# Sketched attention and a squared-ReLU FFN on one core: query features turned in place instead of sent through DRAM

## The chip, the cores and the metric

The kernel runs on one core of a Trainium2 chip. The metric is the device time of one execution in microseconds (us), from several runs of the same kernel, of which the median counts. One further execution was taken by the hardware profiler. Engines: PE multiplies matrices, DVE and ACT are the two engines that can read PSUM and do elementwise work, POOL (GpSimd) works on SBUF alone, SP issues DMAs. DMAs are issued from the queues of SP, ACT and POOL.

## What is computed

There are 4 batch elements with 4 heads, 1088 tokens and a head dimension of 32. A row x has features phi(x): the outer product of S1 x (8 numbers) and S2 x (8 numbers), so 64 products. The attention is linear in these features, and its output goes through an FFN with a squared ReLU:

```python
def phi(x):
    a = np.einsum('rd,bhsd->bhsr', S1, x)
    b = np.einsum('rd,bhsd->bhsr', S2, x)
    return np.einsum('bhsi,bhsj->bhsij', a, b).reshape(*x.shape[:-1], r * r)
q_p, k_p = (phi(q), phi(k))
kv = np.einsum('bhsf,bhsd->bhfd', k_p, v)
z = np.sum(k_p, axis=2)
num = np.einsum('bhsf,bhfd->bhsd', q_p, kv)
den = np.einsum('bhsf,bhf->bhs', q_p, z)[..., None] + 1e-06
x = (num / den)            # heads side by side: (4352, 128)
h = x @ w_in               # 128 -> 2048
out = np.maximum(h, 0.0) ** 2 @ w_out
```

The attention part is in f32, the FFN in bf16.

## The kernel before, in words

The tokens are cut into nine chunks. Chunks 2b and 2b+1 are 512 tokens each of batch element b; chunk 0 is done in two halves, 0a and 0b; chunk 8 (the "rest") has the last 64 tokens of each element, 256 in all. Token j of a partition row is taken as 34 blocks of 32.

**Keys** (`k_stage`, L470; for element 0 the code at L385 to L424). DVE turns k in 32x32 blocks (L473), PE multiplies it by S1 and S2 (L479, L492), DVE turns the result back into token-major order (L484, L497) and makes the 64 products per token and head, kp (L504 in two instructions of 1024, L510 for the last 64 tokens). `z_stage` (L427) sums the factors for the denominators and gives Wc, a third projection whose product with the first one sums to the denominator. `kv_stage` (L449) multiplies kp by v (L456), copies the result (kvs), transposes it on PE (L466) and copies it to KV. For element 0 two of the products run on POOL.

**Queries, token-major** (`token_major`, L543; elements 0 and 1 and the rest). PE projects q to three sets (L555). ACT copies the first, qa. DVE multiplies it by the third (L563), sums it to the denominators (L566), takes the reciprocal (L567), scales qa by it (L569) and makes the products qo, two instructions of 512 for four groups of 128 tokens (L575). PE transposes qo in 128x128 pieces (L583), ACT copies the result to qp, PE multiplies qp by KV to x (`x_mm`, L535; the matmuls are L539), and ACT or DVE copies x to bf16, xT.

**Queries, compact** (`q_stage`, L622; elements 2 and 3). PE projects q feature-major (L633), the result is copied to qab, and `spread` (L608) stores it to DRAM (db on ACT's queue) and loads it back with every row repeated (QB, in two loads on SP's queue). The denominators come by a multiplication (L644), two PE steps (L650, L666) and a reciprocal (L658); the scaled factor, apr (L670), goes the same road through da to QA. DVE multiplies QA by QB to qp for each of two chunks (L679), and `x_mm` follows.

**FFN** (`f_stage`, L689). For each chunk, PE makes h from x and w_in (L707) into two PSUM buffers of two banks, ACT applies the ReLU to 1024 columns at a time (L710), DVE squares 2048 at a time (L714; in chunks 0a, 0b and 1 it may be ACT), and PE multiplies by w_out into one PSUM bank (L721, or L724 in token-major form for chunks 0a, 0b, 1 and 8). r and g have three buffers each. `store_turned` (L731) has DVE turn the output (L734) and SP store it in four DMAs; `store_rows` and `store_rest` copy it and store it.

**Order.** All of this is written as operations with an engine (or a choice of ACT and DVE), an estimated duration, what they read and write, and due times. `Plan.run` sets an order with these by list scheduling, and the instructions are issued in that order, so that each engine's queue is fixed. Three PSUM banks, t, are shared by all attention work, and early work may take the h banks as well (kind "r"). Ahead of the first FFN matmul, fillers (matmuls of zeros, L814) are put into gaps that the plan sees on PE. The first loads are on SP's queue; w_in, w_out and all later loads are on POOL's, behind the `gate` (L369), a small copy on POOL that waits for the first part of q.

Of the kernel before, what the change touches and what calls it, by code (L numbers as in the profile page):

```python
# [17 lines left out]
class Op:  # L18
    __slots__ = ("eng", "fn", "name", "preds", "succs", "dma", "base", "dl", "allocs", "frees", "n", "start", "end", "lead", "pri")
# [6 lines left out]
HOP, DELTA, FIX, TAIL, AHEAD = 0.08, 0.03, 1.4, 0.6, 9.9  # L26
FRAC = 0.94
RATE = 205.0


class Plan:
# [13 lines left out]
    def op(self, eng, dur, fn, reads=(), writes=(), name="", frees=(), dma=None, base=None, lead=0.0, pri=None):  # L45
# [3 lines left out]
        o.frees = list(frees)  # L49
# [40 lines left out]
    def run(self, slots, stretch=1.3, t0=0.7):  # L90
# [7 lines left out]

        left = {o: len(o.preds) for o in self.ops}
        ready = {o for o in self.ops if not o.preds}  # L100
        order = []
        while ready:
            best = {}
            for o in sorted(ready, key=lambda o: o.n):
                if any(not places(t) for t in o.allocs):
                    continue
                slot = max([min(places(t))[0] + HOP for t in o.allocs], default=0.0)
# [23 lines left out]
            if o.dma is not None:  # L131
                q_, x_ = ("SW", "HW") if e == "POOL" else ("HW", "SW")
                begin = max(dmat.get(q_, 0.0), o.end + FIX)
# [8 lines left out]
            for t in o.frees:  # L142
                pool[t.kind].append((s + d, (t.kind, t.i)))
# [19 lines left out]
def kernel(  # L163
# [64 lines left out]
    zs = ring("zs", 2, [128, H, r])  # L228
    KVs = [T(f"KV{b}", [128, 128]) for b in range(B)]
    x0 = T("x0", [128, 512], BF16)  # L230
# [4 lines left out]
    qp = ring("qp", 2, [128, 2, 512])  # L235
    den = ring("den", 2, [128, 32])
# [5 lines left out]
    QA = ring("QA", 2, [128, 2, 1024])  # L242
    QB = ring("QB", 2, [128, 2, 1024])
# [23 lines left out]
    def copy(name, eng, o, i, reads, writes, frees=(), lead=0.0):  # L267
# [4 lines left out]
        op(e, 0, lambda en: act.copy(o(), i()) if en == "ACT" else dve.tensor_copy(o(), i()),  # L272
           reads, writes, name, frees=frees, lead=lead)
# [66 lines left out]
    for i in range(2):  # L340
# [22 lines left out]
        in1=m4[:, None, :, None].to_broadcast([128, 2, H, r]), op=ALU.mult), [tp, "m4"], ["Wab"], "Wab", frees=[tp])  # L363
# [5 lines left out]
    op("POOL", 0.2, lambda e: pool.tensor_copy(gate, Q0[:1, 0, :8]), [f"{Q0k}.0"], ["gate"], "gate", pri=-190.0)  # L369
    load("POOL", "ld w_in", w_in, moe_w_in, 1049, ["w_in"], ["gate"], first=True)  # L370
    load("POOL", "ld w_out", w_out, moe_w_out.rearrange("(c ct) d -> c ct d", ct=CT), 1049, ["w_out"], ["gate"])
# [15 lines left out]
    def k1(m0, m1, Pn, key, nm):  # L387
# [3 lines left out]
        def mm(e):  # L391
            for m in range(n):
# [5 lines left out]
             lambda: pb(t)[:Pn, : 64 * n].rearrange("p (g a i) -> p g a i", a=2, i=r), [t], [f"kabz.{nm}"],  # L398
             frees=[t] if nm == "r" else [])
        for p0 in range(0, n, 2):  # L400
# [3 lines left out]
            def fn(e, p0=p0, p1=p1, w=w):  # L404
# [11 lines left out]
               [f"kabz.{nm}"] + ([] if onp else [t]), [f"{kp0k}.{m0 + p0}"], f"kp0.{m0 + p0}",  # L416
               frees=[t] if p0 == (0 if nm == "0" else 2) and not onp else [])
# [9 lines left out]
    def z_stage(b, keys, feat):  # L427
        t = tmp("r" if b == 0 else "t")

        def mm(e):  # L430
# [9 lines left out]
           [t, "mh"], [zk], f"zs{b}", frees=[t])  # L440
# [3 lines left out]
        copy(f"Wc{b}", "any", lambda: Wt[b][:, 2], lambda: pb(t2)[:, :32], [t2], [f"Wt{b}.c"], frees=[] if b in COMPACT else [t2])  # L444
        if b in COMPACT:
            W_, Wk = WQc(b)
            copy(f"WQc{b}", "any", lambda: W_, lambda: pb(t2)[:, :32].rearrange("p (x c i) -> p c i x", x=2, c=2), [t2], [Wk], frees=[t2])

    def kv_stage(b, parts):  # L449
# [12 lines left out]
        ks, ksk = kvs(b)  # L462
        copy(f"kvs{b}", "any", lambda: ks.rearrange("p (c f) -> p c f", c=2),
             lambda: pb(tv)[:, None, :64].to_broadcast([128, 2, 64]), [tv], [ksk], frees=[tv])
# [76 lines left out]
    ntok = [0]  # L541
# [308 lines left out]
```

## Time and profile before

| what | us |
|---|---|
| median of 3 runs | 125.84 (125.04 to 126.44) |
| the profiled execution, its own time | 124.5 |
| its span, first to last instruction | 122.4 |
| busy: PE, DVE, ACT, POOL | 109.1, 89.5, 84.8, 14.4 |
| first FFN matmul | 16.98 |
| relu, 68 of them (L710) | 66.5 |
| squares on DVE, 32 of them (L714) | 38.8 |
| end of the last FFN matmul | 117.4 |

The granted PE clock was 0.997 of full speed. The DMA queue of SP carried 8.10 MB. The span is the part that the profile's views divide up; 2.1 us of the execution's time lie around it. A group of instructions is named by line, engine, operation and what it writes and reads; the view of waits names the engine that waited, its line, and the engine and line that ended the wait, with the total, the count and the longest.

### The profile page before, as it was taken

The numbers are of one execution on the slowest core, as the hardware profiler recorded it, in microseconds if no ns is written. First come the engines' busy times: TensorE is split into PE (matmuls) and PEld (weight loads), VectorE is DVE, ScalarE is ACT, GpSimd is POOL, SyncE is SP. The second block draws the span as 40 slices with busy tenths as digits, with TensorE's granted clock in tenths as the row PEclk, the third lists the DMA queues.
The fourth block names the chain that finished last, engine by engine and source line by source line (L and its number), as shares of the span: only waits on it lengthen the run. The fifth ranks groups of instructions, "written<-read, shape, count | busy, mean of one in ns | idle before, by whom it ended". The sixth has DMA issues, their size and how long they took to land.

```text
span 122.4 us, 2878 instructions
## 1 busy us (share of the span) xinstructions
PE 109.1 (89%) x1170; PEld 67.7 (55%) x1170; DVE 89.5 (73%) x139; ACT 84.8 (69%) x116; POOL 14.4 (12%) x32
## 2 busy tenths in 40 slices
PE   6999998999998999999994599999979999999530
PEld 4688876947676369663452146455524355547420
DVE  4554797797998669999740999975869896774900
ACT  2431279999799638879779176779893989899510
POOL 3089413310002500000000000000000000000000
PEclk9999999999999999999999999999999999999998
DMA  2999999684013452444499145567950050230051
GB/s 75 270 202 185 247 408 257 137 260 181 12 48 86 124 197 65 110 110 102 105 229 191 45 110 131 111 121 161 200 76 0 0 86 0 35 56 0 16 92 24
DMA packets 19612, 14.88 MB, mean 122 GB/s; under 512 B 13968, under 2 KB 17552, under 8 KB 19088
## 3 DMA queue, kind: packets, MB, share of 16 engines
q1 hardware_dynamic: 17120, 8.10, 31.6%
q0 software_dynamic: 1728, 6.06, 18.0%
q10 hardware_dynamic: 752, 0.55, 1.5%
q8 instruction: 9, 0.15, 0.5%
q14 instruction: 3, 0.02, 0.1%
HBM read 13.00 MB, written 2.75 MB: 129 GB/s over the span
## 4 chain that ended last, share of the span: by engine, by line
PE 40%; DMA 17%; DVE 16%; ACT 13%; issue 10%; DVEq 0%; ACTq 0%
ACT r L710 11%; PE h L707 9%; DMA da<-apr 8%; DVE g L714 7%; PE o_ps L721 7%; PE o_ps L814 7%; DMA QA<-da 6%; PE t L539 3%; PE o_ps L724 3%; DMA out_dram<-osb 2%; DVE kp L504 2%; PE t L555 2%; PE h L456 1%; ACT qp L272 1%; PE t L633 1%
## 5 line engine op out<-in xcount | busy, mean ns | idle before, releaser
L710 ACT ACTIVATE r<-h 128x1024 bf16<-128x1024 f32 x68 | 66.5, 1027 | 11.4 <-PE h L707 11.1
L714 DVE TENSOR_TENSOR g<-r 128x2048 bf16<-128x2048 bf16 x32 | 38.8, 1214 | 7.7 <-ACT r L710 7.6
L707 PE MATMUL h<-xT,w_in 128*128 128x512 bf16 (+1 forms) x128 | 34.3, 371 | 0.5 <-ACT r L710 0.3
L707 PEld LDWEIGHTS <-w_in 128*128 128x128 bf16 x160 | 20.6, 149 | 10.8 <-issue 4.0
L721 PE MATMUL o_ps<-g,w_out 128*128 128x512 bf16 x96 | 24.7, 379 | 0.3 <-DVE g L714 0.2
L721 PEld LDWEIGHTS <-w_out 128*128 128x128 bf16 x96 | 9.0, 97 | 11.8 <-issue 3.2
L539 PE MATMUL t<-qp,KV 64*32 64x512 f32 (+2 forms) x96 | 8.7, 456 | 3.7 <-DVE qp L679 3.7
L724 PE MATMUL o_ps<-w_out,g 128*128 128x128 bf16 x160 | 10.6, 219 | 1.4 <-DVE osb L734 1.2
L724 PEld LDWEIGHTS <-g 128*128 128x128 bf16 x160 | 9.4, 98 | 3.0 <-DVE g L714 1.2
L814 PE MATMUL o_ps<-zero 128*128 128x256 bf16 x47 | 9.0, 335 | 1.2 <-DVE zero L338 1.2
L279 POOL DMA_DIRECT2D vin<-in_v_dram x12 | 6.7, 562 | 21.3 <-PE t L456 13.5
L679 DVE TENSOR_TENSOR qp<-QA,QB 128x1024 f32<-128x1024 f32 x4 | 4.9, 1220 | 5.9 <-DMA QA<-da 4.8
L504 DVE TENSOR_TENSOR kp<-kab 128x1024 f32<-128x1024 f32 x6 | 7.3, 1210 | 0.0
L814 PEld LDWEIGHTS <-zero 128*128 128x128 bf16 x47 | 5.2, 119 | 3.3 <-DVE zero L338 1.2
L575 DVE TENSOR_TENSOR qo<-qaq,t 128x512 f32<-128x512 f32 x9 | 6.0, 684 | 0.2
L734 DVE STREAM_TRANSPOSE osb<-o_ps 128x512 f32<-128x512 f32 x6 | 4.3, 710 | 1.8 <-PE o_ps L721 1.8
L539 PEld LDWEIGHTS t<-qp,KV 64*32 64x32 f32 x96 | 1.8, 105 | 6.9 <-issue 5.0
L583 PE MATMUL t<-ident,qo 128*128 128x128 f32 x32 | 4.8, 278 | 0.2
L707 PE MATMUL h<-x,w_in 128*128 128x256 bf16 x32 | 4.5, 272 | 0.2 <-ACT r L710 0.2
L272 ACT COPY qp<-t 128x512 f32<-128x512 f32 x8 | 4.5, 597 | 0.2 <-PE t L583 0.2
L456 PEld LDWEIGHTS t<-kp,vin 128*32 128x32 f32 (+1 forms) x216 | 3.3, 109 | 2.3 <-issue 2.3
L555 PE MATMUL t<-Wt,qT 128*128 128x96 f32 x32 | 4.5, 279 | 0.0
(107 smaller groups left out, 104.7 us busy)
## 6 DMA issues: line engine op xcount, KB each, us to landing
out_dram<-osb SPq DMA_DIRECT2D x32, 64.0 KB
QB<-db SPq DMA_DIRECT2D x4, 512.0 KB
QA<-da SPq DMA_DIRECT2D x2, 1024.0 KB
kin<-in_k_dram POOLq DMA_DIRECT2D x3, 544.0 KB, 8.3
qin<-in_q_dram POOLq DMA_DIRECT2D x3, 544.0 KB, 4.2
vin<-in_v_dram POOLq DMA_DIRECT2D x6, 144.0 KB, 7.1
vin<-in_v_dram POOLq DMA_DIRECT2D x6, 128.0 KB, 4.7
kin<-in_k_dram SPq DMA_DIRECT2D x2, 256.0 KB
```

The costliest lines, as they stand in the source:

```text
L272: op(e, 0, lambda en: act.copy(o(), i()) if en == "ACT" else dve.tensor_copy(o(), i()), reads, writes, name, frees=frees, lead=lead)
L279: op(eng, 0.5 if eng != "POOL" else 0.8, lambda e: qs[eng].dma_start(out=o, in_=i), reads, writes, name, dma=kb / RATE, pri=seq[0] - 200.0 ...
L504: dve.tensor_tensor(out=kp_[:, 4 * u : 4 * u + 4].rearrange("p m h i j -> p (m h) i j"), in0=x, in1=y, op=ALU.mult)
L539: pe.matmul(o[32 * h : 32 * h + 32, cs], kv_of(b, h), q_[64 * c : 64 * c + 64, x, cs], start=True, stop=True)
L555: pe.matmul(o[p0 : p0 + w, :, g], lhs, Wt[b], start=True, stop=True)
L575: dve.tensor_tensor(out=qo_[:, y : y + 2].rearrange("p g h i j -> p (g h) i j"), in0=x_, in1=y_, op=ALU.mult)
L707: pe.matmul(hv[:, x], w_inv[:, ct], X, start=True, stop=True)
L710: op("ACT", ACT(1024), lambda e, hv=hv, Rv=Rv, u=u: act.activation(Rv[:, KT * u : KT * u + KT], hv, ACTF.Relu), [f"h{hh}"], [f"{Rk}.{u}"], ...
L714: lambda e, R=R, G=G: dve.tensor_mul(G, R, R) if e == "DVE" else act.activation(G, R, ACTF.Square),
L721: pe.matmul(ob[:, :N], w_out[:, ct], Gv[:, y], start=(ct == 0), stop=(ct == CT - 1), skip_group_check=True)
L724: pe.matmul(ob[:, 128 * tt : 128 * tt + 128], Gv[:, y, tt * 128 : tt * 128 + 128], w_out[:, ct], start=(ct == 0 and tt == 0), stop=(ct == ...
L814: pe.matmul(ob[:, :256], zero[:, :128], zero[:, :256], start=True, stop=True)
```

## The change

Elements 1, 2 and 3 all take a new road, `turned_element`; `q_stage` is called no more, so db, da, QA and QB are gone.

- Features are made token-major as before, in two halves of four groups. Instead of PE's transposes and ACT's copies, DVE turns qo in 32x32 blocks into qd (`turned`), one instruction of 1024 for a half.
- x comes from `x_turned`: on 32x32 tiles of PE, four row groups (32 tokens each of a group of 128) by four column groups (heads), the 64 features in two parts that add up in PSUM. It works in two parts u, each with two row groups v, which write to two PSUM banks; each bank is copied to half of one chunk. This needs KV with its features repeated for the four row groups, KV4, made by two PE transposes. The tokens of an element's two chunks are thereby interleaved, and the stores are changed to match: eight DMAs of 32 KB a chunk instead of four of 64 KB.
- The rest takes this road too (REST4); it has a matmul for each group of 32 tokens. Element 0 gets KV4 beside KV.
- Key products of elements 1 to 3 (kp) all run on POOL: four instructions of 512 and one of 256 for the last tokens. kv is issued in four pieces instead of two.
- The first half of chunk 0 (`first_part`) makes its products without the denominators. These are computed beside it, spread by PE (R0.0), copied to Rs by ACT, and multiplied into x on the way out of PSUM, on DVE.
- The gate waits for the second part of k, and no longer for q.
- The plan: new constants and due times; a PSUM buffer is free when its last user has run, instead of at an operation that names it; fillers are put only into gaps of more than 0.07.

```diff
-HOP, DELTA, FIX, TAIL, AHEAD = 0.08, 0.03, 1.4, 0.6, 9.9
-FRAC = 0.94
-RATE = 205.0
+HOP, DELTA, FIX, TAIL, AHEAD = 0.08, 0.0, 1.4, 0.6, 10.0
+FRAC = 0.76
+RATE = 235.0
...
-STRETCH, BASE0, STEP = 1.28, 19.0, 10.36
+STRETCH, BASE0, STEP = 2.12, 16.9, 9.57
 TOK = ("0a", "0b", "1", "8")
 SQA = ("0a", "0b", "1")
-COMPACT = (2, 3)
-LEAD = [12.9, -0.6, -0.4, -0.9, 1.7, 4.2, 2.2, -3.0, 3.3]
+COMPACT = ()
+TURNED = (1, 2, 3)
+KPP = 5
+REST4 = True
+LATE = True
+LEAD = [10.9, -1.2, -0.8, 11.5, 3.0, 3.7, 3.5, -2.5, -15.0]
...
-    op("POOL", 0.2, lambda e: pool.tensor_copy(gate, Q0[:1, 0, :8]), [f"{Q0k}.0"], ["gate"], "gate", pri=-190.0)
+    op("POOL", 0.2, lambda e: pool.tensor_copy(gate, K0[:1, 4, :8]), [f"{K0k}.1"], ["gate"], "gate", pri=-190.0)
...
+        if blocks:
+            k4, k4k = kvs4(b)
+            copy(f"kvs4{b}", "any", lambda: k4,
+                 lambda: pb(tv)[:, :64].rearrange("p (y f) -> p y f", y=2)[:, :, None, :].to_broadcast([128, 2, 4, 32]),
+                 [tv], [k4k])
...
+        def turn4(e):
+            for y in range(2):
+                pe.transpose(pb(t4)[:, 128 * y : 128 * y + 128], k4[:, y].rearrange("p c f -> p (c f)"), ident)
...
-            op("DVE", DVE(1024), fn, [kbk], [f"{kpk}.{4 * u}"], f"kp{b}.{4 * u}")
+            op(*(("POOL", 1.12) if u < KPP else ("DVE", DVE(512))), fn, [kbk], [f"{kpk}.{2 * u}"], f"kp{b}.{2 * u}")
...
-        op("DVE", DVE(256), fnr, [krk], [f"{kpk}.8"], f"kp{b}.8")
+        op(*(("POOL", 0.64) if KPP > 4 else ("DVE", DVE(256))), fnr, [krk], [f"{kpk}.8"], f"kp{b}.8")
         z_stage(b, [kbk, krk], lambda m, a: (kr[:, a] if m == 8 else kb_[:, a, m]))
-        kv_stage(b, [([0, 1, 2, 3], f"{kpk}.0"), ([4, 5, 6, 7], f"{kpk}.4")])
+        kv_stage(b, [([m, m + 1], f"{kpk}.{m}") for m in range(0, 8, 2)])
...
+    def first_part(X, Xk):
...
+        op("DVE", DVE(512), fn, [qak, t], [f"{qok}.0", f"{qok}.2"], "qo0.0")
...
+        op("PE", 0.5, lambda e: x_mm(pb(tx), 0, q_, slice(0, 256)), [f"{qk}.0", "KV0"], [tx], "x0.0")
...
+        op("PE", 0.46, lambda e: [pe.matmul(pb(t3)[32 * h : 32 * h + 32, 128 * g : 128 * g + 128], dn[:, 4 * g + h : 4 * g + h + 1].to_broadcast([128, 32]), ident,
+                                            start=True, stop=True) for g in range(G) for h in range(H)], [dnk, "ident"], [t3], "R0.0")
+        copy("Rs0.0", "ACT", lambda: Rs, lambda: pb(t3)[:, :256], [t3], ["Rs"])
+        op("DVE", DVE(256), lambda e: dve.tensor_tensor(out=X, in0=pb(tx)[:, :256], in1=Rs, op=ALU.mult), [tx, "Rs"], [Xk], "xT0.0")
...
+    def turned(nm, qo_, keys, g0, G):
+        qd_, qdk = qd(0)
+        op("DVE", DVT(256 * G), lambda e: dve.transpose(
+            qd_[:, g0 : g0 + G].rearrange("p g f t -> p (g f t)"), qo_[:, :G].rearrange("p g h x y -> p (g h x y)")),
+           keys, [f"{qdk}.{g0}"], f"qd{nm}")
+        return f"{qdk}.{g0}"
+
+    def x_turned(nm, G, elem, qks, outs, lead):
+        qd_, _ = qd(0)
+        bs = sorted({elem(rg, g) for rg in range(4) for g in range(G)})
+        one = len(bs) == 1
+        n = 32 * G
+        for u in range(2):
+            banks = [tmp(), tmp()]
+
+            def part(e, u=u, banks=banks):
+                for g in range(1 if one else G):
+                    for y in range(2):
+                        for v in range(2):
+                            rg = 2 * u + v
+                            rows = slice(32 * rg, 32 * rg + 32)
+                            for h in range(H):
+                                o = pb(banks[v])[32 * h : 32 * h + 32, :n]
+                                pe.matmul(o if one else o[:, 32 * g : 32 * g + 32], KV4[elem(rg, g)][rows, y, 32 * h : 32 * h + 32],
+                                          qd_[rows, :G, 2 * h + y, :] if one else qd_[rows, g, 2 * h + y, :],
+                                          start=(y == 0), stop=(y == 1))
+
+            op("PE", (0.11 * G + 0.1) if one else 0.5, part, qks + [f"KV4{b}" for b in bs], banks, f"x{nm}.{u}")
+            for v in range(2):
+                X, Xk = outs[v]
+                copy(f"xT{nm}.{'AB'[v]}{u}", "any", lambda X=X, u=u: X[:, n * u : n * u + n], lambda v=v, banks=banks: pb(banks[v])[:, :n],
+                     [banks[v]], [f"{Xk}.{u}"], lead=lead)
+
+    def turned_element(b):
+        qt, qtk = qT(b)
+        keys = []
+        for u in range(2):
+            parts = [(g, 0, qt[:, 512 * u + 128 * g : 512 * u + 128 * g + 128], b) for g in range(4)]
+            qo_, ks_ = token_major(f"{b}.{u}", parts, 4, None, None, ([(b, None, None)], [(0, 0, f"{qtk}.{x}") for x in range(3)]), "turned")
+            keys.append(turned(f"{b}.{u}", qo_, ks_, 4 * u, 4))
+        x_turned(str(b), 8, lambda rg, g: b, keys, [xT(2 * b), xT(2 * b + 1)], LEAD[2 * b])
...
+                for x in range(4):
+                    for u in range(2):
+                        load("SP", f"st o{nm}.{x}{u}", o[:, u, :, 32 * x : 32 * x + 32], osv[32 * x : 32 * x + 32, u], 0.3 * N, [], [ok])
...
-                while t is not None and t < o.start < first + 0.01:
+                while t is not None and t + 0.07 < o.start < first + 0.01:
                     pe.matmul(ob[:, :256], zero[:, :128], zero[:, :256], start=True, stop=True)
-                    t += 0.22 if t < 4.5 else 0.11
+                    t += 0.215 if t < 5.5 else 0.11
```

More of the change, by code (lines that the diff above doesn't have):

```diff
@@ L132, in run @@
                 q_, x_ = ("SW", "HW") if e == "POOL" else ("HW", "SW")
-                begin = max(dmat.get(q_, 0.0), o.end + FIX)
+                begin = max(dmat.get(q_, 0.0), o.end + (1.0 if o.pri is not None else FIX))
                 shared = min(max(dmat.get(x_, 0.0) - begin, 0.0), 2 * o.dma) / 2
@@ L228 @@
     zs = ring("zs", 2, [128, H, r])
+    kvs4 = ring("kvs4", 2, [128, 2, 4, 32])
     KVs = [T(f"KV{b}", [128, 128]) for b in range(B)]
+    KV4 = [T(f"KV4{b}", [128, 2, 128]) for b in range(B)]
     x0 = T("x0", [128, 512], BF16)
@@ L265, in DVT, with copy @@
         return 0.18 + n * 0.00104
-    def copy(name, eng, o, i, reads, writes, frees=(), lead=0.0):
+    def copy(name, eng, o, i, reads, writes, lead=0.0):
         n = 1
@@ L575, in fn @@
                 dve.tensor_tensor(out=qo_[:, y : y + 2].rearrange("p g h i j -> p (g h) i j"), in0=x_, in1=y_, op=ALU.mult)
[L577 removed]
+            op("DVE", DVE(512), fn, [qqk, t], [f"{qok}.{y}"], f"qo{nm}.{y}")
+        if kind == "turned":
+            return qo_, [f"{qok}.{y}" for y in range(0, G, 2)]
         q_, qk = qp(i_)
```

185 lines of the change are left out of this document (129 added, 56 removed).

## The prediction

> **What bounds the kernel now.** I read three views in this order: busy time in ten equal stretches from the first FFN matmul (17 us) to the last (117.5 us), then who waited for whom, then the chain that ended last. Columns of the first: the stretch and its length, busy us (and instructions) of PE, PE weight loads, DVE, ACT and POOL, granted clock, DMA share, GB/s.
>
> ```profile
> 47.00:57.00 10.00, 10.00 (x127) 6.49 (x125) 9.86 (x15) 8.42 (x13) 0.00 (x0) 1.00 0.45 106
> 57.00:67.00 10.00, 8.59 (x92) 4.23 (x89) 4.62 (x9) 8.18 (x10) 0.00 (x0) 1.00 0.76 166
> 67.00:77.00 10.00, 8.02 (x52) 4.00 (x56) 9.56 (x13) 5.06 (x10) 0.00 (x0) 1.00 0.45 98
> ...
> sum 100.50, PE 93.32 PEld 55.50 DVE 79.47 ACT 79.21 POOL 6.08; mean PE 9.33 PEld 5.55 DVE 7.95 ACT 7.92 POOL 0.61
> ```
>
> PE is busy 93.3 of 100.5 us, DVE and ACT 79 each. A busy PE need not be a working PE, so I checked the sum from the chain, where four 512-column FFN matmuls take 0.86. The FFN is 8.5 chunks of 32 such matmuls, 272 x 0.215 = 58.5; keys, queries and x add about 34. That makes 93: the busy time is real work, and PE is the bound. Of its 7.2 us idle, 3.4 lie between 57 and 77.
>
> ```profile
> DVE qp L679 <- DMA QA<-da: 4.8, 1, 4.8
> PE t L539 <- DVE qp L679: 3.7, 2, 3.0
> DVE qp L679 <- DMA out_dram<-osb: 1.1, 1, 1.1
> ```
>
> ```profile
> 49.88 9.76 DMA da<-apr
> 59.65 7.67 DMA QA<-da
> ```
>
> The last lines are of the chain, in order of time (start, us, what): the first round trip stores da at 49.88, loads QA from 59.65, and lands at 67.3. It holds PE for 3.0 us, the second (its product at 89.8) for 0.7. PE cannot make this up, since it has little idle time elsewhere.
>
> **The change part by part.** All durations are of the profiled execution: span 122.4, own time 124.5, so 2.1 lie around the span. The median of the three runs, 125.84, is 1.1% above that.
>
> Round trips. For elements 2 and 3 the compact query stage goes, with four 128 KB stores, four 512 KB and two 1 MB loads. PE's waits for them end: -3.7. Their transfers lie beside compute otherwise; SP's and ACT's queues lose ten issues of about 0.55 each.
>
> PE work, in throughput from the chain. Removed: for element 1 two halves of 0.97 (features), 0.9 (eight 0.11 transposes) and 1.0 (x), 5.7; for elements 2 and 3, 1.0 + 0.62 + 0.5 + 0.44 + 2 x 1.0 = 4.55 each, 9.1; rest chunk 0.48 + 0.45 + 0.58 = 1.5. Sum 16.3. Added: features 6 x 0.97 = 5.8. The x of an element is two parts of 32 instructions (every logical f32 matmul is two) of 256 columns on 32x32 tiles. By the key projection's row, 16 instructions of 256 columns on four column groups in 1.0, one of them costs 0.25 alone, 0.0625 with four abreast, 0.031 with eight. The nearest row for two row groups is x now: eight instructions of 512 columns on 64x32 tiles in 0.99, four abreast, upper and lower rows together but never on the same columns. The new form has two row groups on the same columns into different banks. Bounds: 1.0 a part if they run together, 2.0 if they take turns, so 5.9 or 11.8 for six. I take 5.9, because the row shows upper and lower rows at work together at full rate; the other end is a rival. The rest's x becomes 128 instructions of 32 columns; the nearest row, 64 instructions of 64 columns in 1.03 (kp with vin), is bound by issue at 16 ns, so 2.1. Rest features 0.5. KV4 turns twice 0.11 instead of once in three elements and additionally in element 0: +0.7. Added 15.0, net -1.3. The Trainium skill, page TensorEngine Tiling (Array Packing), Key Properties and Gotcha 1, says that distinct tiles work in parallel and that row tiles must write different banks at one time; the new code does, so by that rule the sum keeps the 5.9. It also says that a change of tiling mode drains the engine; no row here separates such a drain, and the x of today changes mode as often.
>
> DVE. Removed: key products 6 x 1.21 + 3 x 0.41 = 8.5; of the compact stage 4.0 an element (two products 1.22, and 0.42, 0.35, 0.29, 0.42), 8.0; one 0.23. Added: four token-major halves of 0.28 + 0.30 + 0.25 + 0.29 + 2 x 0.68 = 2.5, 10.0; block turns 6 x 1.22 + 0.71 = 8.0 (row of qT, 128x1024 in 1.22). Net +1.3. ACT: copies of qp 5 x 0.6, qab 2 x 0.59, WQc 2 x 0.19 and den 0.2 go, qa 4 x 0.27 and Rs 0.37 come: -3.3. On either: x leaves in 256-column copies (6 of 0.58 become 12 of 0.37 to 0.42, one of 0.41 becomes four of 0.2), KV4 copies are wider and element 0 has two more: +2.9. DVE and ACT together go from 158.7 to 159.6, 80 each against PE's 92. Priced at nothing on the path: PE covers them; without that cover the +0.9 would be shared by two engines.
>
> POOL. Twelve products of 1.06 and three of 0.62 (the two POOL rows of L411) make 14.6, 4.9 for an element, against 2.8 on DVE, where they were spread from 28.5 to 36.6 for element 1. POOL's queue holds them in order with the loads, and a v load waited 11.1 for PE there; a product placed behind such a load waits too, and kv, x and F1 behind it. POOL has 14.4 busy of 122.4, so room is there. The latency costs between 0 (as quick as DVE's spread) and +3 (the whole excess of 2.0 for the first element, which has least lead, and 0.5 for each other); I take 0, because DVE's own spread has kv of element 1 at 35.0 to 39.4 and the x that needs it at 41.9. Such products beside squares on DVE are not in the trace; that is the last rival. The nearest row is POOL's 1.06 product beside a DVE product of 0.69, both undisturbed.
>
> The start.
>
> ```profile
> 14.33 0.27 ACT L272 COPY KV<-t 128x128 f32<-128x128 f32 x1 [0.43 <-PE t L466]
> ...
> 14.56 0.60 PE L583 MATMUL h<-ident,qo 128*128 128x128 f32 x4
> ...
> 15.20 0.58 ACT L272 COPY qp<-h 128x512 f32<-128x512 f32 x1 [0.49 <-PE h L583]
> ...
> 15.96 0.64 PE L539 MATMUL h<-qp,KV 64*32 64x256 f32 x8
> ...
> 16.66 0.37 ACT L272 CAST x<-h 128x256 bf16<-128x256 f32 x1 [0.29 <-PE h L539]
> ```
>
> KV is there at 14.60, but x waits until 15.96 for qp, whose chain begins with the denominators. Now qo is made without them, some 1.1 earlier (0.22 + 0.23 + 0.20 + 0.23, with the gaps), so x can begin at 14.65; its end 15.29 and a product of 0.42 bring F1 to about 15.8 instead of 17.0: -1.2. The denominators' own road (c, three DVE steps, R, a copy of 0.37, about 2.5 from 11.0) ends before. Fillers: nine run between 10.5 and 17, four of 0.22 each between the kv steps on the path; a gap under 0.07 no longer gets one: between 0 and -0.9, I take -0.4. The gate now waits for k instead of q, so that w_in starts up to 1.2 earlier and shares the engines with q and v; v was there at 10.5 when kv needed it, and I price it at 0 with an upper bound of +1.
>
> The end. Chunk 7 stores in eight pieces instead of four. SP took 115.05 to 117.0 for four and was free at 117.79 for the last chunk's four. At 0.32 (the shortest) to 0.5 (the median) eight take 2.6 to 4.0, so the last ones begin 0 to 1.2 later: +0.4. In other chunks the extra issues lie beside everything. The plan's constants and the freeing of PSUM banks move the order only; x now takes two of three banks at once. Bounds: -3.5 (all other idle time of PE) to +3.5 (the same again); I take 0.
>
> Sum: 122.4 - 3.7 - 1.3 - 1.2 - 0.4 + 0.4 = 116.2 span, 118.3 own time, times 125.84/124.5 = 119.6 on the scale of the median.
>
> **The rivals.**
> 1. Row groups on the same columns take turns: +5.9 on PE, 125.5. For it: no row shows them together. Against it: x now.
> 2. The order tightens as well, since no transfer has to be waited out: PE's other 3.5 go too, 116.1. For it: 1.8 of these lie after 107, where little attention work is left beside the relus, and work that ends later would fill them. Against it: ACT's relus fill 9.1 of 10 us from 97 on.
> 3. A queue takes the wait over: POOL's products behind a v load, or x for two free banks. +3, 122.6. For it: POOL's 13.5 us of waits for kv. Against it: they fell where POOL had nothing else to do.
> 4. Slower: POOL's products and DVE's squares exclude each other. Both inputs of a square are in SBUF, and there are 32 squares of 1.21 on the way from relu to F2. If a square started during a product is held to its end, DVE loses up to 14.6, and PE with it once the three r and g buffers are used up. It decides from 7.5 on the path, half of it (6.2 gained and 1.3 for the 1%); with three quarters, 10.9, the time is 130.5. Against it: POOL's load issue of 0.55 at 24.8, inside a square that took 1.19. That is no product, though. The Trainium skill, page SBUF — State Buffer, Who interferes with whom, states just this lock for a VectorE instruction with two SBUF inputs against a GpSimd instruction that reads SBUF; no run here shows it yet.
>
> **How the numbers follow.** Forecast (117 to 122) 0.47; rival 1 0.09; rival 2 0.19; rival 3 0.12; rival 4 0.13. A measurement here tells about 1% from no change: under 124.6 is faster, over 127.1 slower. Faster: forecast, 2, 3 and a third of 1, whose 125.5 lies within 1%: 0.81. Same: the rest of 1 and the mild part of 4: 0.08. Slower: 0.11. The range reaches from below rival 2 (1 us for the start's bounds) to just past rival 1: 115.0 to 126.0, leaving out rival 4 and little below.
>
> **What would show it.** Right: no da, db, QA, QB; PE's wait for qp gone and nothing of 3 us in its place; first F1 before 16; q1 down from 8.1 MB by about 4; x of an element at 1.0 a part; DVE's squares still at 1.21 while POOL multiplies; the last store within 1.2 us of its place now. Wrong: an x part of 2.0 (rival 1), POOL products or squares stretched or started late against each other (rival 4), PE waiting for kp behind a v load (rival 3), or DVE busy over 90% from 17 on.

## The result and the profile after

| | before | after |
|---|---|---|
| median of 4 runs each | 125.51 (125.04 to 126.44) | 122.06 (120.23 to 123.61) |
| ratio | | 0.961 [0.949, 0.974] |
| profiled execution: own time, span | 124.5, 122.4 | 122.79, 121.0 |
| first FFN matmul | 17.09 (its weights from 16.98) | 15.44 |
| last copy of the output ends | 117.76 | 114.57 |
| from there to the end of the span | 4.64 | 6.43 |

The change makes the kernel about 4% faster by the ratio and 2.7% by the medians; 119.6 was forecast, a ratio of 0.95. The ratio is formed from each kernel's executions within 1.5% of its fastest; the profiled one of after, at 122.79, is not among them, so its views show where time can go and not what the executions behind the ratio hold.

In the code of after, the relu is L848, the square L852, the FFN matmuls L845, L859 and L862, the key products L539 (512 each) and L546, the features L591, the x of the turned elements L716 and a copy through the helper L291.

First the waits of after: engine and line that waited, who ended the wait, total us, times, longest.

```profile
POOL kp L539 <- DVE kab L519: 18.6, 2, 16.6
...
PE t L591 <- DVE Wt L291: 2.1, 1, 2.1
PE o_ps L862 <- DVE g L852: 2.0, 4, 0.7
...
PE h L845 <- ACT r L848: 1.8, 7, 0.5
```

PE's wait of 3.7 for qp is gone, and the queue that carried the round trips is half as full (packets, MB, share of the DMA engines; before, then after):

```profile
q1 hardware_dynamic: 17120, 8.10, 31.6%
...
q1 hardware_dynamic: 16872, 3.90, 15.5%
```

But a new wait stands in its place: 2.1 us for Wt, which PE never waited for before. The groups say where to look (the first line is of before, the others of after; count, busy us, mean ns, idle before):

```profile
L714 DVE TENSOR_TENSOR g<-r 128x2048 bf16<-128x2048 bf16 x32 | 38.8, 1214 | 7.7 <-ACT r L710 7.6
...
L852 DVE TENSOR_TENSOR g<-r 128x2048 bf16<-128x2048 bf16 x33 | 44.5, 1356 | 6.7 <-ACT r L848 6.6
...
L539 POOL TENSOR_TENSOR kp<-kab 128x512 f32<-128x512 f32 x12 | 16.3, 1385 | 18.6 <-DVE kab L519 18.6
```

A square took 1214 ns on average before and takes 1356 now; a product of POOL, 1059 alone, takes 1385. Neither writes what the other reads. The timeline (start, length, engine, line, instructions joined) shows the worst case:

```profile
23.33 4.14 POOL L539 TENSOR_TENSOR kp<-kab 128x512 f32<-128x512 f32 x4
...
25.08 4.07 DVE L852 TENSOR_TENSOR g<-r 128x2048 bf16<-128x2048 bf16 x1
...
27.45 0.61 POOL L546 TENSOR_TENSOR kp<-kabr 64x256 f32<-64x256 f32 x1
...
29.07 0.18 DVE L291 COPY Wt<-t 128x32 f32<-128x32 f32 x1
...
29.30 2.02 PE L591 MATMUL t<-Wt,qT 128*128 128x96 f32 x16 [2.13 <-DVE Wt L291]
```

One square, 1.2 us of work, lasts 4.07: it is asked for while POOL runs its row of products and ends 1.1 after the last of them, so it began its own work only when the row was over. The copy of Wt, which PE needs for the features of element 1, is behind it on DVE's queue, and PE runs dry. In the later rows of products, squares and products take turns (squares of 1.82 to 1.87), and PE waits 0.37 behind one of them, at 43.5. In ten stretches, with the columns of the prediction's first view, the largest hole is here:

```profile
25.40:35.40 10.00, 7.87 (x105) 5.52 (x103) 9.64 (x16) 5.40 (x8) 3.25 (x5) 1.00 0.52 164
...
sum 98.80, PE 92.39 PEld 58.13 DVE 84.54 ACT 77.32 POOL 24.11; mean PE 9.24 PEld 5.81 DVE 8.45 ACT 7.73 POOL 2.41
```

PE has 6.4 us idle, 2.1 of them in this stretch. Finally the x of a turned element, from the chain in order of time (start, us, instructions):

```profile
44.58 1.02 PE t L716 x32
```

The 32 instructions of a part take 1.02, the lower of the two bounds.

### The profile page after: what moved, and what is told of

Read it like the earlier page. It is cut to its first block, busy times and chain, and to the rows that moved or that the text cites. A ratio compares the mean times of both kernels' runs of the same rounds, so it can differ in the third digit from the quotient of the medians.

```text
span 121.0 us, 3319 instructions
## 1 busy us (share of the span) xinstructions
PE 106.3 (88%) x1361; PEld 68.6 (57%) x1361; DVE 93.2 (77%) x149; ACT 83.0 (69%) x120; POOL 32.4 (27%) x47
## 4 chain that ended last, share of the span: by engine, by line
PE 57%; ACT 10%; DVE 9%; DMA 8%; issue 8%; ACTq 1%; SPq 0%; DVEq 0%
PE h L845 19%; PE o_ps L859 16%; ACT r L848 9%; PE t L591 5%; PE t L716 5%; DMA qin<-in_q_dram 5%; PE o_ps L862 5%; DVE g L852 4%; DMA S2r<-in_S_dram 3%; PE t L473 3%; PE t L514 2%; DVE qo L611 2%; DVE kT L508 1%; ACTq L298 1%; PE t L450 1%
## 5 line engine op out<-in xcount | busy, mean ns | idle before, releaser
L848 ACT ACTIVATE r<-h 128x1024 bf16<-128x1024 f32 x68 | 66.6, 1025 | 10.5 <-PE h L845 9.6
L852 DVE TENSOR_TENSOR g<-r 128x2048 bf16<-128x2048 bf16 x33 | 44.5, 1356 | 6.7 <-ACT r L848 6.6
L845 PE MATMUL h<-xT,w_in 128*128 128x512 bf16 (+1 forms) x128 | 34.6, 370 | 1.7 <-ACT r L848 1.6
L845 PEld LDWEIGHTS <-w_in 128*128 128x128 bf16 x160 | 20.4, 147 | 11.9 <-issue 5.3
L859 PE MATMUL o_ps<-g,w_out 128*128 128x512 bf16 x96 | 24.7, 379 | 0.0
L539 POOL TENSOR_TENSOR kp<-kab 128x512 f32<-128x512 f32 x12 | 16.3, 1385 | 18.6 <-DVE kab L519 18.6
L859 PEld LDWEIGHTS <-w_out 128*128 128x128 bf16 x96 | 8.9, 98 | 10.1 <-issue 1.1
L862 PE MATMUL o_ps<-w_out,g 128*128 128x128 bf16 x160 | 10.6, 219 | 2.0 <-DVE g L852 2.0
L862 PEld LDWEIGHTS <-g 128*128 128x128 bf16 x160 | 9.4, 98 | 3.4 <-DVE g L852 2.8
L611 DVE TENSOR_TENSOR qo<-qaq,t 128x512 f32<-128x512 f32 x16 | 10.3, 678 | 0.1
L591 PE MATMUL t<-Wt,qT 128*128 128x96 f32 x60 | 7.8, 280 | 2.4 <-DVE Wt L291 2.1
L591 PEld LDWEIGHTS t<-Wt,qT 128*128 128x128 f32 x60 | 7.2, 191 | 3.6 <-DVE Wt L291 2.7
L716 PE MATMUL t<-qd,KV 32*32 32x256 f32 (+1 forms) x320 | 8.1, 307 | 0.0
L693 DVE STREAM_TRANSPOSE qd<-qo 128x1024 f32<-128x1024 f32 (+1 forms) x7 | 7.8, 1147 | 0.0
L291 ACT CAST xT<-t 128x256 bf16<-128x256 f32 (+2 forms) x13 | 4.6, 380 | 3.7 <-PE t L716 3.6
L291 ACT COPY qta<-t 128x128 f32<-128x128 f32 (+1 forms) x10 | 2.5, 249 | 6.0 <-PE t L591 4.6
L716 PEld LDWEIGHTS t<-qd,KV 32*32 32x32 f32 x320 | 4.2, 104 | 3.6 <-issue 2.4
L970 PE MATMUL o_ps<-zero 128*128 128x256 bf16 x25 | 5.1, 363 | 1.2 <-DVE zero L357 1.2
L473 PE MATMUL t<-kp,vin 128*32 128x64 f32 (+1 forms) x216 | 5.3, 224 | 0.0
```

What stands on the lines that cost most here:

```text
L473: pe.matmul(pb(tv)[32 * h : 32 * h + 32, :64], V[:Pn, h, m, :], kp_[:Pn, m, h].rearrange("p i j -> p (i j)"), start=(m == 0), stop=(m == 8 ...
L539: (pool if e == "POOL" else dve).tensor_tensor(out=kp_[:, 2 * u : 2 * u + 2].rearrange("p m h i j -> p (m h) i j"), in0=x, in1=y, op=ALU.mult)
L591: pe.matmul(o[p0 : p0 + w, :, g], lhs, Wt[b], start=True, stop=True)
L611: dve.tensor_tensor(out=qo_[:, y : y + 2].rearrange("p g h i j -> p (g h) i j"), in0=x_, in1=y_, op=ALU.mult)
L693: op("DVE", DVT(256 * G), lambda e: dve.transpose(qd_[:, g0 : g0 + G].rearrange("p g f t -> p (g f t)"), qo_[:, :G].rearrange("p g h x y - ...
L716: pe.matmul(o if one else o[:, 32 * g : 32 * g + 32], KV4[elem(rg, g)][rows, y, 32 * h : 32 * h + 32], qd_[rows, :G, 2 * h + y, :] if one ...
```

## The experiments

The theory after the result: the gain is the round trips' and the start's, and two things took part of it back, squares held by POOL's reads (the prediction's rival 4, in part) and a longer end. The rivals: POOL slows DVE in some way other than by its reads, or the products are simply late; and the spread of the times has a cause of its own in the start. The kernels ran in three sets, each on one chip and beside before, whose medians were 124.70, 124.11 and 124.61: the first set is again to stores4, the second fill_old to trips, the third the rest. Times are us; the first is the profiled execution's.

**again: the kernel of after, unedited.**

> The changed kernel once more, unedited. Its four runs so far spread from 120.2 to 123.6, wider than those of the kernel before (125.0 to 126.4). Theory A (the long squares are squares that wait for a POOL product): the same few squares are stretched again, between 1.8 and 4.1 us, and the number of long ones changes from run to run, so that the spread stays over 1.5 us. Theory B (the stretch is chance in one profile): other squares or none are long, and the spread is as small as before. Time by both: 121 to 123, a ratio of 0.96 to 0.975.

125.14, 121.51, 120.08, 126.84, 120.23, 126.79, 123.31; ratio 0.970 [0.964, 0.976]. Before's fourteen lie between 123.8 and 126.0. The gain repeats in the better executions; by the medians it is 1.1% here (123.31 against 124.70). The spread of single executions repeats too and is far wider than before's. In the profiled one the square is held for 4.95, and the stretches after it show a second loss (granted clock third from the end):

```profile
28.00:30.00 2.00, 0.00 (x0) 0.00 (x0) 2.00 (x1) 0.45 (x1) 1.09 (x2) 1.00 0.75 235
30.00:32.00 2.00, 1.67 (x13) 1.67 (x13) 2.00 (x5) 0.27 (x1) 0.08 (x1) 0.87 0.28 87
32.00:34.00 2.00, 2.00 (x16) 1.99 (x16) 1.54 (x5) 0.27 (x1) 0.51 (x1) 0.50 0.50 111
```

PE has nothing to do for 3.0 us, and soon after works at half the clock until about 35. In the profile of after, with 2.1 idle, the clock held.

**kp_fill: two fills in place of each product on POOL.** The order of the instructions stays.

```diff
-                (pool if e == "POOL" else dve).tensor_tensor(out=kp_[...], in0=x, in1=y, op=ALU.mult)
+                for _ in range(2):
+                    pool.memset(kp_[...], 0.01)
...
```

> POOL's key products of elements 1 to 3 are left out; in their place POOL writes constants to kp, two fills for each product, so POOL is busy at the same places and reads nothing from SBUF. The order of every engine is that of the changed kernel. Theory A (squares and products shut each other out through reads of SBUF): all squares take 1.18 to 1.25, the 3.4 us hole of DVE near 25 us and PE's 2.1 us wait behind it go, and the time falls by 1.5 to 3.5 against the changed kernel in the same call. Theory B (what delays DVE there is its order, not POOL): no square changes by more than 0.3 and the time stays within 1.

119.97, 123.23, 125.38, 120.04, 122.57, 127.48; ratio 0.965 [0.959, 0.971].

```profile
L852 DVE TENSOR_TENSOR g<-r 128x2048 bf16<-128x2048 bf16 x33 | 39.7, 1210 | 6.4 <-ACT r L848 6.2
```

POOL is as busy in the same place (24.22 to 28.5), now only writing, and every square is back at 1.2 (longest 1226 ns). The wait for Wt is gone. So POOL at work with products, which read SBUF, holds DVE, and POOL at work with fills does not, as the first theory had it. The Trainium skill, page SBUF — State Buffer, Who interferes with whom, says that a VectorE instruction with two SBUF inputs contends with a GpSimd instruction that reads SBUF and not with one that only writes it; the trace agrees, 1356 against 1210 ns. But the best executions are no faster than those of again (119.97 against 120.08), and some at 123 to 127 remain, so the hold is not all of the spread.

**kp_dve: the products on DVE, at the same places.**

```diff
-            o.fn(e)
+            o.fn("DVE" if e == "POOL" and o.name[:2] == "kp" and o.name[:3] != "kp0" else e)
```

> The key products of elements 1 to 3 run on DVE at the places in the order where POOL had them; nothing else changes. Four of 0.68 and one of 0.41 an element, 9.4 more on DVE. Theory A: no square is long any more (4.4 us back), but DVE has 5 us more net; it is busy 89 to 90 of 99 and PE waits more: 0 to +3 us against the changed kernel. Theory B (POOL cost DVE nothing): DVE has 9.4 more, +4 to +7 us.

123.0, 125.36, 122.9, 122.94, 125.03, 123.88, 124.33, 122.5, 124.39; ratio 0.988 [0.983, 0.993]. Squares are at 1211 ns, DVE is busy 87.5 of 99.4 us, and PE waits 1.1 for Wt and 0.7 for zs. The best executions are 2.4 above those of again. POOL's products are thus worth having: what they save on DVE is more than the hold takes in the better executions.

**stores4: four stores of 64 KB a chunk instead of eight of 32.** The copies of x put the tokens in order already.

```diff
-                    for u in range(2):
-                        load("SP", f"st o{nm}.{x}{u}", o[:, u, :, 32 * x : 32 * x + 32], osv[32 * x : 32 * x + 32, u], 0.3 * N, [], [ok])
+                    load("SP", f"st o{nm}.{x}", o[:, :, 32 * x : 32 * x + 32], osv[32 * x : 32 * x + 32], 0.6 * N, [], [ok])
...
```

> Four stores of 64 KB a chunk instead of eight of 32 KB: the copies of x put their columns into the order of tokens, so that each store is one access pattern again. The order of every engine is kept. Theory A (the longer end comes from SP's queue: the last chunk's four stores follow eight others closely, and the DMA engines still have those to write): the time from the end of the last copy of the output to the end of the span falls from 6.4 to about 4.6 as before the change, -1.5 to -2. Theory B (the end is the landing of the last store, whatever comes ahead): 6 us or more remain, and the time stays within 0.5. The copies of x to 64-byte runs may cost up to 0.1 each, off the path.

128.35, 120.08, 126.46, 120.24, 120.82, 120.81; ratio 0.969 [0.965, 0.973], as again. From the last copy to the end it is still 6.1, as in again with its eight stores. The theory that SP's longer queue of stores makes the end late falls. The profiled execution has something else to show, its first key matmuls (the first two lines are of after, the next two of stores4):

```profile
5.03 1.00 PE L413 MATMUL h<-Wab,kT 128*128 128x64 f32 x8
...
5.87 1.32 PE L413 MATMUL t<-Wab,kT 128*128 128x64 f32 x10
```

```profile
5.12 1.80 PE L413 MATMUL h<-Wab,kT 128*128 128x64 f32 x8
...
6.72 2.32 PE L413 MATMUL t<-Wab,kT 128*128 128x64 f32 x10
```

The same matmuls take 1.8 times as long, and the first FFN matmul comes at 22.92 instead of 15.4. The views give the granted clock as 1.00 all this time, but they count 1.00 where the trace has no clock record, and its first record, of a full clock, is at 24.2 here and at 4.9 in after. At 24.2 the FFN matmuls go from 0.21 apart to 0.11 apart. So this is a start in which PE got its full clock 19 us late.

The profile shows one thing more. The square that is held in after asks 0.8 into a product here, and it gets the next turn (1.32), before the third product (2.05):

```profile
32.16 1.06 POOL L539 TENSOR_TENSOR kp<-kab 128x512 f32<-128x512 f32 x1
...
32.98 1.32 DVE L852 TENSOR_TENSOR g<-r 128x2048 bf16<-128x2048 bf16 x1
...
33.19 2.05 POOL L539 TENSOR_TENSOR kp<-kab 128x512 f32<-128x512 f32 x1
```

**fill_old: the fillers of before.**

```diff
-                while t is not None and t + 0.07 < o.start < first + 0.01:
+                while t is not None and t < o.start < first + 0.01:
...
-                    t += 0.215 if t < 5.5 else 0.11
+                    t += 0.22 if t < 4.5 else 0.11
```

> The changed kernel with the fillers of the kernel before: eight more matmuls of zeros ahead of the first FFN matmul, every other order kept. In the changed kernel some executions take 120.1 to 120.3 and others 122.5 to 128.4, and in the profile of one of 128.35 every PE instruction from 5 to 23 us takes twice its time (key projection 1.80 for eight instead of 1.00), though the instructions are the same. Theory A (PE's clock is still low because fewer fillers keep it busy in the start, and it depends on chance when it rises): with the fillers back no execution is above 125, the spread falls below 3, and the start is later by 0 to 0.9. Theory B (the slow executions come from the loads): the spread stays at 6 or more.

124.39, 121.96, 121.8, 120.84, 125.18, 120.93, 121.62; ratio 0.975 [0.968, 0.982]. The first FFN matmul comes at 16.61. The eight profiles with the thinner fillers and no late clock have it at 15.3 to 16.0, so these fillers are worth 0.6 to 1.3. The highest time is just over the 125 that the theory on the start allowed and the spread is 4.3, so it is not settled by this run. The square is held in the profile as before the edit (PE waits 2.6), although it asks only 0.25 into a product:

```profile
26.00 1.07 POOL L539 TENSOR_TENSOR kp<-kab 128x512 f32<-128x512 f32 x1
...
26.25 4.54 DVE L852 TENSOR_TENSOR g<-r 128x2048 bf16<-128x2048 bf16 x1
```

**kp_gap: a fill of 8 columns between the products.**

```diff
...
+                pool.memset(gap, 0.0) if e == "POOL" else None
...
```

> A fill of 8 columns in a scratch tile stands ahead of each of POOL's twelve products of 512, so that POOL writes for about 0.1 us between two products and reads nothing; the order is kept. Theory A (a square that waits for the product gets its turn only when POOL's row of products is broken): the long square near 25 us falls from 4.1 to at most 2.3, PE's wait behind it from 2.1 or 3.0 to under 0.5, and fast executions come 1 to 2.5 sooner than the 120.1 of the changed kernel. Theory B (the square waits for the products whatever stands between them): it stays at 4 or gets longer by the fills, and the time stays.

126.89, 119.96, 119.92, 120.2, 128.1, 126.46; ratio 0.964 [0.956, 0.971].

```profile
24.53 1.08 POOL L539 TENSOR_TENSOR kp<-kab 128x512 f32<-128x512 f32 x1
...
25.30 5.17 DVE L852 TENSOR_TENSOR g<-r 128x2048 bf16<-128x2048 bf16 x1
25.54 0.11 POOL L539 MEMSET gap<- 128x8 f32 x1
25.60 1.07 POOL L539 TENSOR_TENSOR kp<-kab 128x512 f32<-128x512 f32 x1
```

The square asks 0.8 into the first product, a fill of 0.11 follows, and the square is still held until the row is over. The products start 1.07 apart, against 1.03 in after, so the fill breaks the row for some 0.04 only. A stop this short doesn't hand the turn over; a longer one was not tried. PE idles 3.2 and the clock is at 0.50 from about 30 to 37.

**rest_st: the last four stores with 32 partitions as their outer count instead of 2.**

```diff
-        o = out.rearrange("(tt b t j) d -> b j tt t d", tt=2, b=2, j=NJ)
+        o = out.rearrange("(tt b t j) d -> b tt t j d", tt=2, b=2, j=NJ)
...
-                load("SP", f"st o8.{bb}{v}", o[bb, 32 + v], osv[64 * bb : 64 * bb + 64, v], 32, [], [ok])
+                load("SP", f"st o8.{bb}{v}", o[bb, v, :, 32:], osv[64 * bb + 32 * v : 64 * bb + 32 * v + 32], 32, [], [ok])
```

> The last chunk's four stores take 32 partitions with 1 KB a row each instead of 64 partitions with 512 bytes, so that the outermost count on the DRAM side is 32 and not 2; nothing else changes. Four stores ahead instead of eight left the end at 6.1 us, so the queue is not what made it longer. Theory A (each of these stores runs on few of the DMA engines since its outer count is 2, as the profile's 0.11 to 0.14 share and 32 to 44 GB/s for three us suggest): the time from the last copy to the end falls from 6.1 to 6.4 to 4.7 or less, -1.5. Theory B (the landing takes this long for any store after a closely packed row): it stays above 5.8.

124.24, 119.82, 124.4, 120.42; ratio 0.965 [0.955, 0.974]. The times say nothing that the spread does not cover; the end in the profile does. Stretches of 1 us from 2.0 behind the last copy on, the last columns being clock, DMA share and GB/s, of after and then of rest_st:

```profile
116.60:117.60 1.00, 0.00 (x0) 0.00 (x0) 0.00 (x0) 0.00 (x0) 0.00 (x0) 0.98 0.14 44
117.60:118.60 1.00, 0.00 (x0) 0.00 (x0) 0.00 (x0) 0.00 (x0) 0.00 (x0) 0.50 0.14 41
118.60:119.60 1.00, 0.00 (x0) 0.00 (x0) 0.00 (x0) 0.00 (x0) 0.00 (x0) 0.50 0.11 32
```

```profile
120.30:121.30 1.00, 0.00 (x0) 0.00 (x0) 0.00 (x0) 0.00 (x0) 0.00 (x0) 1.00 0.16 39
121.30:122.30 1.00, 0.00 (x0) 0.00 (x0) 0.00 (x0) 0.00 (x0) 0.00 (x0) 0.92 0.00 0
```

After moves its last bytes for 3 us at 0.11 to 0.14, the work of some two DMA engines out of 16; in rest_st nothing moves any more in the second stretch. The end, 6.1 to 6.4 so far, falls to 4.2, below before's 4.64. Before's last stores had the 32 tokens outermost; the change made it two token halves. The edit also makes rows of 1 KB out of rows of 512 bytes, but before's rows had 512 bytes too, so their length isn't the cause. The Trainium skill, page DMA: Bandwidth & Descriptors, section "Why a DMA increments its semaphore by 16 and not by 1", says that a DMA uses as many engines, up to 16, as divide the outermost counts of both its sides; for an outer count of 2 that is two engines, and the trace agrees.

**trips: the round trips back in.** Elements 2 and 3 take the compact road of before within the kernel of after, planned anew.

```diff
-COMPACT = ()
-TURNED = (1, 2, 3)
+COMPACT = (2, 3)
+TURNED = (1,)
```

> The round trips come back alone: elements 2 and 3 take the compact stage through DRAM, element 1, the rest, POOL's key products, the start and the plan stay as in the changed kernel (the order is planned anew, with half of the constants' fit lost). Theory A (the waits for the round trips cost 3.7 as priced): PE waits 2 to 4 us for the products again, and fast executions take 122.5 to 125. Theory B (the start and the order carry the gain, the round trips could be hidden): PE's wait for the products is under 1 and the time is within 1 of the changed kernel's 120.1 to 121.5.

141.38, 135.89, 142.04, 138.67. This tells nothing of the price of the round trips: PE waits for none of their products here, but a kernel 16 us slower than before has room to hide them. The plan's constants do not fit the mixed order (DVE waits 20.1 for relus, against 6.6), and the profile has the slow start of stores4 as well.

**sq_act: the square that is held goes to ACT.**

```diff
-            o.fn(e)
+            o.fn("ACT" if o.name == "sq 0b.0" else e)
```

> One square moves: that of the second half of chunk 0 which waited for POOL's row of products (4.1 to 5.2 us in five profiles) is done by ACT, at the same place in the plan, 1.9 us; ACT is busy 5.4 of the ten us there. Everything else is the changed kernel. Theory A (this one wait empties PE, and when PE is empty for 3 us its clock is halved for the next 6 us, which makes the executions of 122.5 to 125): PE's wait of 2.1 to 3.2 for Wt goes, no stretch between 27 and 45 has a granted clock under 0.9, fast executions take 117.5 to 119.5, and the middle group goes; only executions with a slow start (126 and more) may remain. Theory B (PE is bound anyway and other waits take its place): fast executions stay at 119.8 to 120.5.

120.16, 122.61, 121.18, 120.31, 119.72, 120.22; ratio 0.964 [0.959, 0.970]. The stretch from the first FFN matmul to the last:

```profile
15.30:111.70 96.40, 92.12 (x1178) 58.12 (x1177) 80.59 (x123) 78.70 (x102) 24.10 (x26) 1.00 0.30 68
```

PE has no wait for Wt, the clock is never under full, DVE is busy 80.6 instead of 84.5 (1.2 of the difference is the square's own work, now on ACT), and the last copy ends at 112.09, 2.5 earlier than in after's profile. The times spread over 2.9 instead of 6.8, though best2 below, with the same edit, spreads over 6.8 again. And the best of them are no better than the best of again: 119.7 to 120.3, where 117.5 to 119.5 was expected. So the hold explains the profile of after, and hardly its best executions; how long it lasts in those was not seen.

**notrip: before, with the round trips left out and nothing else.** QA and QB hold constants.

```diff
-        op(eng, ..., lambda e: qs[eng].dma_start(out=o, in_=i), reads, writes, name,
+        op(eng, ..., lambda e: None if name[:4] in ("st a", "st b", "ld Q") else qs[eng].dma_start(out=o, in_=i), reads, writes, name,
...
+            if o.name == "ld kin_0.2":
+                [pool.memset(x(i)[0], 0.5) for x in (QA, QB) for i in range(2)]
```

> The kernel before with its round trips left out and nothing else changed: no stores to da and db, no loads to QA and QB; these hold a constant that POOL writes once, so that elements 2 and 3 are computed from constants. Theory A (the term of the prediction): the waits of 3.0 and 0.7 go and nothing takes their place, 120 to 121.5, -2.5 to -4 against the kernel before in this call. Theory B (PE's time is filled by other waits, as in the changed kernel, where PE's idle time fell by 0.8 only): -1 or less.

118.84, 119.8, 119.94, 120.01 against 124.61 (123.93 to 126.89); ratio 0.959 [0.953, 0.965]. Again from the first FFN matmul to the last:

```profile
16.30:112.00 95.70, 92.79 (x981) 55.34 (x979) 79.52 (x110) 79.05 (x97) 9.89 (x16) 1.00 0.27 65
```

Without its round trips the old kernel is as fast as the best executions of the new one, and PE's idle time in this stretch falls from 7.2 to 2.9. The round trips, waits and transfers together, are worth 4.7 us of the median, more than the 2.5 to 4 expected, and everything else in the change comes to nothing on balance.

**best1 and best2: sq_act, rest_st and stores4 together**, best1 with the fillers of before, best2 with those of after.

> The changed kernel with four edits: the square on ACT, the last chunk's stores of 32 partitions, four stores a chunk, and the fillers of the kernel before. Theory A (the hold, the end and the clock at the start are separate losses and add up): the end after the last copy at 4.5 or less, no PE wait of over 1 us in the start of the FFN, the first FFN matmul at 16 to 16.7, fast executions 116 to 118.5 and none above 121. Theory B (they overlap): fast executions stay above 119.

> The same without the fillers of the kernel before, so with those of the changed kernel. Theory A (the fillers decide the slow starts, and cost 0.5 to 1.1 otherwise): fast executions come 0.5 to 1 sooner than with them, 115.5 to 118, but some of the executions take 5 to 8 more, with PE at half speed up to 23 us. Theory B (the slow executions have another cause): the spread is the same with and without.

best1: 123.48, 120.4, 121.38, 119.96, 119.03, 120.25; ratio 0.961 [0.955, 0.968]. best2: 118.96, 121.7, 118.72, 119.25, 124.95, 118.2; ratio 0.952 [0.945, 0.959]. best2 is the fastest version, with a median of 119.11 against 124.61 for before, and its profile ends 4.1 after the last copy. The best executions, 119.03 and 118.2, fall short of what was expected if the losses add up (116 to 118.5 and 115.5 to 118). The slow start is in best1's profile (first FFN matmul at 20.13, first clock record at 13.8) in spite of the old fillers, so it doesn't take the thinner fillers to bring it.

## Why the prediction was right, and where it was wrong

To set the steps against numbers, the span is cut at the first FFN matmul and at the end of the last copy. Beside after stand sq_act, where the square isn't held, and notrip:

| us | before | after | sq_act | notrip |
|---|---|---|---|---|
| start, to the first FFN matmul | 17.1 | 15.4 | 15.3 | 16.3 |
| middle, to the end of the last copy | 100.7 | 99.1 | 96.8 | 96.1 |
| end | 4.6 | 6.4 | 6.3 | 4.2 |
| span | 122.4 | 121.0 | 118.4 | 116.6 |

- **Round trips, -3.7: right, and too small.** The middle of notrip is 4.6 shorter than before's. The wait of PE was the price on the path, and the 3.0 us hole was not given back elsewhere, as the view of stretches had said.
- **The start, -1.2 and -0.4: right in sum.** It is 1.6 shorter. The split is less sure: fill_old puts 0.6 to 1.3 of that on the fillers, where 0.4 was taken with a bound of 0.9, so 0.3 to 1.0 is left for the products made without denominators. The gate may have taken some back, which was not tested: w_in is now loaded sooner, and DVE waits 2.8 for q's second part, priced at 0 with a bound of +1. Single profiles of one start differ as well: notrip has before's and needs 16.3.
- **The x parts, 1.0 each: right.** 1.02 in the chain; rival 1 falls.
- **PE work, -1.3: about half of it seen, and none of it in the time.** PE's sum is 92.4 in after and 92.1 in sq_act, near the 92.0 of the forecast, but in notrip, where none of before's matmuls was removed, it is 92.8. So 0.5 of before's 93.3 was waiting that counts as busy, and 0.4 to 0.7 is left as saved work. By its rows it should have been more than 1.3: the rest's x took 1.4 (two parts of 0.68 in the chain) where 2.1 was priced, and five more transposes of 0.11 for KV4 make 0.55, not 0.7. The middle of sq_act is no shorter than notrip's all the same, since PE is idle for 4.3 in it and for 2.9 in notrip.
- **The end, +0.4: the step that was mis-sized.** It measures +1.8. Eight issues instead of four were counted and the change to the shape of the last four stores was overlooked: stores4 shows that the issues cost 0.3 at most, rest_st that the shape costs about 2.
- **POOL at 0: the step that failed in the profile.** The latency of the products was priced, their effect on DVE was left to rival 4. That rival came true in one place: a square held for 4 to 5 us, PE idle for 2 to 3, and in three of the five profiles with it a half clock for 3.4 to 6.8 us behind it. It costs the profiled execution 2.4 (99.1 against 96.8). It stayed far below the rival's 10.9, because only one square was held for a whole row; three others lost 0.65 each, and cost PE one wait of 0.37. DVE's sum shows the size: +1.3 was forecast and +5.1 came, and what these four squares took beyond 1.2 makes 4.8.
- **The order at 0.** In time that was right within the 0.7 between sq_act and notrip. Rival 2 did not come: 4.3 us of PE's idle time remain in sq_act. Rival 3 did not come either: POOL's waits behind loads (5.6 at most) delay no product that PE waits for; its waits name no kp.

The executions that the ratio rests on are 4.8 below before, where 6.2 were forecast. By the table, -4.6 for the trips and -1.6 for the start less 1.8 at the end leave -4.4, so the sum was right in the main for the reason given, the round trips. The miss of 1.4 is just what the end was short, and that is partly luck: the 0.9 that the trips gave beyond their price stands against PE work that brought no time.

Longer executions have more: the held square, the half clock behind it, or the slow start. That the change brings the hold is shown (kp_fill and sq_act take it away). How much of it the best executions have is not known, since every profile that shows it is of a longer one. The slow start is PE's full clock coming at 13.8 to 24.2 us instead of 3.9 to 6.1. What delays it is open: it came with old and new fillers alike, and the one profile of before doesn't show it.

## What to carry to other kernels

Before work is moved to GpSimd, see which two-input DVE instructions will run beside it, and what stands behind them on DVE's queue: the held square itself cost little here, but the small copy behind it, which PE needed, cost PE 2 to 3 us. When a layout changes, read the outermost count of every DMA that stores it, above all of the last ones, which nothing covers. Leaving out one part of the old kernel (notrip) prices that part better than putting it back into the new one (trips), whose order was made without it.

## What was not expected of the hardware

- A DVE square that asks for SBUF while POOL runs a row of products can be held until the row is over: 4.07 to 5.17 us for 1.2 of work in five profiles, through three to five products. At other times it gets the next turn (1.32 in stores4, 1.82 to 1.87 in the later rows), and the product behind it takes up to 2.05. How far into a product it asks does not decide: it was held after 0.18 (rest_st) and 0.25 (fill_old), and served after 0.8 (stores4). The DMA engines were 0.84 to 0.92 busy during the held squares and 0.07 at most during those that got the next turn; whether that plays a part was not tested. A write-only instruction of 0.11, which moved the products 0.04 apart, changed nothing.
- After 3.0 and 3.2 us without a matmul the granted clock fell to 0.50, for 3.4 us (again) and 6.8 us (kp_gap); after 2.1 (after) and 2.6 (fill_old) it did not. rest_st had 2.2 and fell all the same, and before had 3.0 behind its round trip and kept the full clock, so the length of the idle time alone doesn't tell.
- PE can stay at about half rate for the first 14 to 24 us although it is kept busy (best1, trips and stores4; 4 to 6 us in the other eleven profiles). The views then give a granted clock of 1.00, because the trace has no clock record for that time: the row's own durations (1.80 against 1.00 for eight matmuls) are the better witness.
